# Last tile's stores of a fused attention and MLP kernel: two groups of 64 rows per transfer, the left columns of one half on their own

## The chip, the cores and the metric

The kernel runs on one core of a Trainium2 chip. The metric is device time: the microseconds that one execution takes on that core, as the median of three runs.

## The reference, cut to what matters

Efficient attention, then a two-layer MLP. `q`, `k` and `v` are float32 of shape (8, 8, 576, 64): batch, heads, sequence, head dimension. Per batch and head

- `q_s` is the softmax of `q` over the head dimension, `k_s` the softmax of `k` over the sequence;
- `kv = k_s^T v` (64 x 64), and the attention output is `q_s kv`.

The heads are laid side by side, which gives `x` of 4608 tokens by 512. Then `h = x w_in` (512 to 2048), `g = max(0.01 h, h)`, and the output is `g w_out` (2048 to 512): 4608 x 512 float32, 9.44 MB.

## The kernel before, in words

**Tiles.** The 4608 tokens are worked in nine tiles of 512 (`TT`). For each tile the attention output, transposed, is the right operand of layer 1; its result goes through the leaky ReLU and is the left operand of layer 2, whose result stands with tokens on the 128 partitions and 512 output columns. From tile 1 on layer 2 uses a scheme of seven products of half-size blocks in place of eight; tiles 7 and 8 use it for both layers. Each product is accumulated in PSUM by TensorE (`behind`, L922) and the quarters of the output are sums of products: some are kept in SBUF by ScalarE (`q...` words, L987 and L989), and the last addition of each quarter is one VectorE TENSOR_TENSOR that writes the output tile (`total`, L871).

**Order.** The order of the instructions is written out by hand: `SCORE` is a list of words for tiles 1 to 6, `WEAVE` (L816) one for tiles 7 and 8, and `of_tile` (L933) turns a word into instructions. Each engine runs its own instructions in that order; a semaphore holds one back until what it needs is done. The last words of `WEAVE` are

```
d21 P310 d22 d11 d120 P311 d121
```

`P310` and `P311` are the two halves of the last product for the second 128 rows. `d21`, `d22`, `d11`, `d120` and `d121` are the final sums on VectorE. The first digit behind the `d` names the half of the tile (2 is the second 256 rows, 1 the first), the second the columns (1 is the left 256, `low`; 2 the right 256, `high`). `d120` and `d121` are the right columns of the first half, split by 128 rows, because they wait for the last product.

**The output tile.** `rows_out(t, c)` is a float32 tile of 128 partitions x 2 x 512 for half `c` of tile `t`: the middle index (`sub`) is the group of 128 tokens, the partition is the token within it. Tokens are ordered by `(r, l)` within a batch, `r` one of 9 and `l` one of 64, and token `(r, l)` is row `9 l + r` of the batch in DRAM. So the 128 partitions of a `sub` hold two groups of 64 rows (`i` = 0 and 1: partitions 0 to 63, and 64 to 127), and a group's 64 rows lie 9 rows of 2,048 bytes apart in DRAM.

**Stores.** `put` (L724, its DMA at L728) stores a half of a tile: one DMA for each `sub` and each `i`, 64 rows of 2,048 bytes, 128 KB. In the last tile (`t == NT - 1`, tile 8) `issue` (L1007) gives the DMAs of `i` = 0 to SyncE (SP) and those of `i` = 1 to ScalarE (ACT); in the other tiles all go to SP. For the last tile the calls are

- at L1003, as soon as `d21` and `d22` are both issued: four stores for the second half (c = 1);
- at L992, after `d120` and again after `d121`: two stores each, for one `sub` of the first half (c = 0), whole rows. `d11` has already written the left columns of both.

That is eight stores, four on SP and four on ACT. Behind them in each queue stands only the end of the program (L1112 for the compiler's closing waits), where SP waits for every DMA to land before all engines sign off.

Of the kernel before, what the change touches and what calls it, by code (L numbers as in the profile page):

```python
# [19 lines left out]
L = 64  # L20
# [5 lines left out]
def kernel(  # L26
# [13 lines left out]
    B, H, S, D = q.shape  # L40
# [9 lines left out]
    TT = 512  # L50
# [673 lines left out]
    def put(t, osb, c, os, subs=both, issue=(nc.sync, nc.sync)):  # L724
        for sub in subs:
            for i in range(2):
# [2 lines left out]
                    out=out_r[b, r0 // L, :, os], in_=osb[c][i * L : (i + 1) * L, sub, os]  # L729
                )  # L730

    spare = {}

    def spare_tile(key, shape, dtype):
# [120 lines left out]
    def rows_out(t, c):  # L855
        if (t, c) not in ot:
            ot[t, c] = osb_pool.tile([P, 2, O], FP32, name="out_sb")
        return ot[t, c]
# [74 lines left out]
    def of_tile(t, word):  # L933
        kind, p = word.split("_")[0], int(word[-1])
        k0 = word[0]
        out_bank = lambda x, i=0: bank[x, t, "out", i][0]
        if k0 == "u":
            j = int(word[1]) * NK + p
            c0 = L if t == 1 else 0
            bank["U", t, j] = psB_pool.tile([P, TT - c0], FP32, name="ph", tag=BANK_TAG)  # L940
            layer1(j, bank["U", t, j], t * TT + c0, TT - c0)
        elif k0 == "l" and "_" not in word:
            h = int(word[1])
            leaky(g_of(t, p // 2)[:, h, p % 2, L if t == 1 else 0 : TT], bank["U", t, h * NK + p])
        elif k0 == "m":
            ahead(t, int(kind[1]), p)
        elif k0 == "P" and len(word) == 3:
            s, p = int(word[1]), int(word[2])
            if p == 0:
                bank["O", t, s] = psO_pool.tile([P, O], FP32, name="pout")  # L950
            for i in range(4 * p, 4 * p + 4):
                layer2(bank["O", t, s], [g_of(t, kk) for kk in range(p + 1)], s, ORDER[i], i == 0, i == NF - 1)
        elif k0 == "P":
            behind(t, *(int(c) for c in word[1:]))
        elif k0 == "s":
            nc.scalar.copy(out=fill(t, kind, p), in_=bank["Z" if kind == "s5" else "X", t, p])  # L956
        elif k0 == "c":
            x, held = {"c11": ("Y", "s1"), "c22": ("X", "s5"), "c12": ("Z", "s6")}[kind]
            held = empty(t, held, p)
            total(fill(t, kind, p), bank[x, t, p], held)  # L960
        elif k0 == "l":
            z = {"l11": "a1", "l12": "a2", "l21": "b1", "l22": "b2"}[kind]
            if kind == "l11" and t >= WOVEN:
                c = empty(t, "c11", p)
                nc.vector.scalar_tensor_tensor(
                    out=corner(t, p, z), in0=c, scalar=LEAKY_SLOPE, in1=c, op0=ALU.mult, op1=ALU.max
                )
            else:
                leaky(corner(t, p, z), bank["X", t, p] if kind == "l21" else empty(t, "c" + kind[1:], p))
        elif k0 == "n":  # L970
            i = int(kind[1])
            h = p if t in PAIRED else p // 2
            if (t, h, i) not in nt:
                nt[t, h, i] = sum_pool.tile([P, 2, 2, HT], BF16, name=f"gs{i + 1}{h}")
            if t in PAIRED:
                o, (x, y) = nt[t, h, i], (corners(t, h, z) for z in SUB[kind])
            else:
                o, (x, y) = nt[t, h, i][:, place(t, p)], (corner(t, p, z) for z in SUB[kind])
            nc.vector.tensor_tensor(out=o, in0=x, in1=y, op=ALU.subtract)  # L979
        elif word == "q21":  # L980
            nc.scalar.copy(out=rows_out(t, 1)[:, :, low], in_=out_bank("X"))
        elif k0 == "q":
            i = int(word[1])
            if (t, i) not in keep:
                keep[t, i] = fill(t, word, 0) if i == 4 else keep_tile(i)
            if len(word) == 3:
                nc.scalar.copy(out=keep[t, i][:, p : p + 1], in_=out_bank("Z", p))  # L987
            else:
                nc.scalar.copy(out=keep[t, i], in_=out_bank({1: "X", 4: "V", 5: "Z", 6: "X"}[i]))  # L989
        elif word in ("d120", "d121"):  # L990
            total(rows_out(t, 0)[:, p : p + 1, high], out_bank("Z", p), keep[t, 6][:, p : p + 1])
            put(t, {0: rows_out(t, 0)}, 0, whole, [p], issue(t))  # L992
        elif k0 == "d" and len(word) == 2:
            o = rows_out(t, p // 2)[:, p % 2]
            move(nc.scalar if p < 2 else nc.vector, o, bank["O", t, p])
        elif k0 == "d":
            c, os, x, i = {"11": (0, low, "Y", 1), "12": (0, high, "Z", 6), "22": (1, high, "X", 5), "21": (1, low, "X", 4)}[word[1:]]
            total(rows_out(t, c)[:, :, os], out_bank(x), keep[t, i])
            if i == 4:
                empty(t, "q4", 0)  # L1000
            made[t, word] = True
            if t >= WOVEN and c == 1 and (t, "d21") in made and (t, "d22") in made:
                put(t, {1: rows_out(t, 1)}, 1, whole, both, issue(t))  # L1003
        else:
            put(t, {p: rows_out(t, p)}, p, whole)

# [110 lines left out]
```

## Time and profile before

| | us |
|---|---|
| median of 3 runs | 268.75 (268.65 to 268.89) |
| the profiled execution | 268.51 |
| its span, first to last recorded instruction | 266.7 |
| TensorE busy in the span | 256.2 (96%) |
| VectorE, ScalarE busy | 223.1, 193.1 |

The granted TensorE clock was 0.995 over the span. The profiled execution is 0.24 us below the median of the three runs, and 1.8 us of it lies outside the span.

A row of the timeline or of a group gives start and duration in us, the engine, the line of the kernel, the operation, and the tiles (out<-in) with their shapes and count. "SPq" and "ACTq" rows are DMA issues on the queues of SyncE and ScalarE: their duration is that of the issuing instruction, not of the transfer. The DMA view of a stretch has two rows of 40 slices (busy share of the 16 DMA engines in tenths, and GB/s), then the packets of each queue: q1 is SP's, q10 is ACT's, q14 and q8 are fetches of instructions. The share behind a queue is the sum of its packets' durations over 16 engines times the stretch; packets that start in a stretch count in full, so a share can pass 100%. "Us to landing" is from the start of the issue until the last of the transfer's semaphore counts has come in.

### The profile page before, as it was taken

How to read it: one execution, taken by the hardware profiler on the slowest of the kernel's cores; microseconds unless marked ns; L12 is line 12 of the kernel's file. 1: busy time of each engine (PE TensorE's matmuls, PEld its weight loads, DVE VectorE, ACT ScalarE, POOL GpSimd, SP SyncE). 2: the span in 40 equal slices, each digit the busy share in tenths (PEclk: the TensorE clock that was granted, in tenths of full speed). 3: DMA queues.
4: the chain of work that ended last, by engine and by line, in shares of the span. 5: the costliest groups of instructions: out<-in, count | busy, mean ns of one | idle time of the engine just before them, and what ended most of it. 6: DMA issues, size and time to landing. Idle time of an engine off the chain costs nothing.

```text
span 266.7 us, 6315 instructions
## 1 busy us (share of the span) xinstructions
PE 256.2 (96%) x2559; PEld 188.4 (71%) x2570; DVE 223.1 (84%) x390; ACT 193.1 (72%) x367; POOL 64.2 (24%) x45
## 2 busy tenths in 40 slices
PE   7689999999999999999999999999999999999992
PEld 3167744457864686458888864588888788888882
DVE  2997899699999999989798969786999579779952
ACT  4977893689579769797469766878996589628920
POOL 2484442160038100000930191058000000000000
PEclk9999999999999999999999999999999999999998
DMA  7999999996895299299409766463028160042004
GB/s 242 343 210 360 314 209 268 316 327 244 187 396 218 48 240 339 78 179 332 172 4 243 279 187 247 95 81 75 2 51 179 41 140 0 2 96 64 1 2 159
DMA packets 37646, 46.49 MB, mean 174 GB/s; under 512 B 18160, under 2 KB 21232, under 8 KB 37616
## 3 DMA queue, kind: packets, MB, share of 16 engines
q1 hardware_dynamic: 32976, 36.64, 47.7%
q0 software_dynamic: 4320, 8.91, 13.4%
q10 hardware_dynamic: 320, 0.52, 0.6%
q8 instruction: 20, 0.33, 0.5%
q14 instruction: 10, 0.08, 0.1%
HBM read 36.70 MB, written 9.44 MB: 173 GB/s over the span
## 4 chain that ended last, share of the span: by engine, by line
PE 84%; DMA 6%; ACT 2%; DVE 1%; issue 1%; POOL 0%; ACTq 0%; POOLq 0%
PE acc L922 37%; PE ph L491 29%; PE ph L892 14%; DMA w_in_sb<-in_moe_w_in_dram 3%; DMA qX<-qe 3%; PE po L436 2%; PE pkv L294 2%; ACT ke L201 1%; DVE k_raw L378 1%; PE pout L516 1%; ACT vb L211 1%; ACT qe L264 0%; POOL w_in_sb L129 0%; DVE out_sb L871 0%; POOL gate L574 0%
## 5 line engine op out<-in xcount | busy, mean ns | idle before, releaser
L491 PE MATMUL ph<-xT,w_in_sb 128*128 128x256 bf16 (+3 forms) x505 | 85.8, 325 | 0.8 <-DMA w_in_sb<-in_moe_w_in_dram 0.2
L491 PEld LDWEIGHTS <-w_in_sb 128*128 128x128 bf16 x512 | 49.6, 98 | 32.9 <-issue 0.6
L500 ACT ACTIVATE gj<-ph 128x512 bf16<-128x512 f32 (+2 forms) x116 | 60.7, 573 | 15.5 <-PE ph L491 10.8
L922 PEld LDWEIGHTS <-gs 128*128 128x128 bf16 x512 | 49.5, 98 | 7.0 <-issue 1.0
L256 POOL TENSOR_TENSOR q_raw<-q_raw,qmax 128x2304 f32<-128x2304 f32 (+3 forms) x10 | 30.8, 3086 | 89.3 <-ACT xT L427 55.2
L922 PEld LDWEIGHTS <-gj 128*128 128x128 bf16 x384 | 37.3, 98 | 6.1 <-issue 0.4
L922 PE MATMUL acc<-w_out_sb,gj 128*128 128x256 bf16 x256 | 32.2, 273 | 0.0
L922 PE MATMUL acc<-wsum,gs 128*128 128x256 bf16 x256 | 30.6, 273 | 0.0
L922 PE MATMUL acc<-w_out_sb,gs 128*128 128x256 bf16 x256 | 30.4, 273 | 0.0
L979 DVE TENSOR_TENSOR gs<-gj 128x512 bf16<-128x512 bf16 (+1 forms) x56 | 24.6, 456 | 1.9 <-ACT gj L500 1.7
L871 DVE TENSOR_TENSOR part_spare<-ph,part_spare 128x512 f32<-128x512 f32 x36 | 23.5, 686 | 2.8 <-PE ph L892 2.5
L979 DVE TENSOR_TENSOR gs<-gj,gs 128x512 bf16<-128x512 bf16 (+1 forms) x56 | 24.7, 458 | 0.9
L956 ACT COPY part_spare<-ph 128x512 f32<-128x512 f32 x36 | 19.3, 592 | 8.1 <-PE ph L892 7.7
L427 ACT CAST xT<-po 128x320 bf16<-128x320 f32 (+2 forms) x47 | 19.0, 482 | 7.9 <-PE po L436 7.6
L871 DVE TENSOR_TENSOR out_sb<-acc,keep 128x512 f32<-128x512 f32 (+1 forms) x26 | 16.5, 645 | 9.3 <-ACT xT L427 6.1
L273 DVE TENSOR_REDUCE qsum<-qe 128x36 f32<-128x2304 bf16 (+4 forms) x11 | 19.7, 1793 | 3.2 <-ACT qe L264 3.1
L264 ACT ACTIVATE qe<-q_raw 128x2304 bf16<-128x2304 f32 (+4 forms) x11 | 16.8, 1526 | 6.8 <-POOL q_raw L256 6.8
L280 DVE TENSOR_TENSOR qe<-qe,qrec 128x2304 bf16<-128x2304 bf16 (+4 forms) x12 | 21.2, 1763 | 0.2
L225 DVE TENSOR_REDUCE qmax<-q_raw 128x36 f32<-128x2304 f32 (+4 forms) x11 | 19.6, 1791 | 1.4 <-DMA q_raw<-in_q_dram 1.4
L989 ACT COPY keep<-acc 128x512 f32<-128x512 f32 x22 | 12.8, 585 | 10.9 <-PE acc L922 9.9
L892 PEld LDWEIGHTS <-fs_spare 128*128 128x128 bf16 x192 | 18.8, 98 | 2.2
L892 PE MATMUL ph<-xs_spare,fs_spare 128*128 128x256 bf16 x144 | 19.2, 273 | 0.0
(86 smaller groups left out, 313.9 us busy)
## 6 DMA issues: line engine op xcount, KB each, us to landing
out_dram<-out_sb SPq DMA_DIRECT2D x68, 128.0 KB, 3.3
q_raw<-in_q_dram SPq DMA_DIRECT2D x6, 1152.0 KB, 8.2
v_raw<-in_v_dram SPq DMA_DIRECT2D x6, 1152.0 KB, 7.9
k_raw<-in_k_dram SPq DMA_DIRECT2D x5, 1152.0 KB, 7.2
w_in_sb<-in_moe_w_in_dram POOLq DMA_DIRECT2D x4, 512.0 KB, 7.9
w_out_sb<-in_moe_w_out_dram POOLq DMA_DIRECT2D x3, 512.0 KB, 16.0
k_raw<-in_k_dram SPq DMA_DIRECT2D x2, 576.0 KB, 5.4
v_raw<-in_v_dram SPq DMA_DIRECT2D x2, 576.0 KB, 7.4
```

Source lines behind the costliest of these rows:

```text
L225: nc.vector.tensor_reduce(out=m, in_=st[b]["q"][:, :, rs], axis=AX.X, op=ALU.max)
L256: eng.tensor_tensor(out=qs, in0=qs, in1=st[b]["qmax", rs.start].unsqueeze(3).to_broadcast([P, HL, n, D]), op=ALU.subtract,)
L273: nc.vector.reduce_sum(out=qsum, in_=st[b]["qe"][:, rs], axis=AX.X)
L280: eng.tensor_tensor(out=qes, in0=qes, in1=st[b]["qrec", rs.start].unsqueeze(3).to_broadcast([P, n, HL, D]), op=ALU.mult,)
L427: eng.copy(out=o, in_=i)
L491: nc.tensor.matmul(ph[:, n0:n1], lhsT=w_in_sb[:, i, j * P : (j + 1) * P], rhs=xT[:, i, (c0 + n0) % NX : (c0 + n0) % NX + n1 - n0], start=( ...
L500: nc.scalar.activation(out=o, in_=ph, func=AF.Prelu, alpha=LEAKY_SLOPE)
L871: nc.vector.tensor_tensor(out=o, in0=x, in1=y, op=ALU.add)
L892: nc.tensor.matmul(bank[x, t, p][:, jj], lhsT=lhs(k, 2 * p + jj), rhs=rhs[:, k], start=(first and k == 0 and jj == 0), stop=(k == 1), skip ...
L922: nc.tensor.matmul(b[:, at_], lhsT=lhs(k)[:, sub * P : (sub + 1) * P], rhs=rhs[:, k], start=(first and k == 0 and at_ == 0), stop=(k % (NK ...
L956: nc.scalar.copy(out=fill(t, kind, p), in_=bank["Z" if kind == "s5" else "X", t, p])
L979: nc.vector.tensor_tensor(out=o, in0=x, in1=y, op=ALU.subtract)
```

## The change

Only tile 8 changes, and only its stores; no sum and no product is touched.

- A new helper `put_both` stores the two subs of a half in one DMA for each `i`: 64 partitions x 2 subs, so both groups of 64 rows that lie on these partitions.
- The second half (c = 1) is stored by two such DMAs of 256 KB, whole rows, in place of four of 128 KB.
- Behind `d11` two DMAs store the left 256 columns of the first half: 64 partitions x 2 subs x 1,024 bytes, 128 KB each.
- The stores behind `d120` and behind `d121` take the right 256 columns alone: 64 rows x 1,024 bytes, 64 KB each, two DMAs each.

There are eight stores before and after, four on each queue.

```diff
+    def put_both(t, osb, c, os, issue):
+        b, r0 = divmod(t * TT + c * HT, S)
+        for i in both:
+            issue[i].dma_start(
+                out=out_r[b, r0 // L + i : r0 // L + i + 3 : 2, :, os].rearrange("r l o -> l r o"),
+                in_=osb[c][i * L : (i + 1) * L, :, os],
+            )
...
         elif word in ("d120", "d121"):
             total(rows_out(t, 0)[:, p : p + 1, high], out_bank("Z", p), keep[t, 6][:, p : p + 1])
-            put(t, {0: rows_out(t, 0)}, 0, whole, [p], issue(t))
+            put(t, {0: rows_out(t, 0)}, 0, high if t == NT - 1 else whole, [p], issue(t))
...
             if t >= WOVEN and c == 1 and (t, "d21") in made and (t, "d22") in made:
-                put(t, {1: rows_out(t, 1)}, 1, whole, both, issue(t))
+                if t == NT - 1:
+                    put_both(t, {1: rows_out(t, 1)}, 1, whole, issue(t))
+                else:
+                    put(t, {1: rows_out(t, 1)}, 1, whole, both, issue(t))
+            if t == NT - 1 and word == "d11":
+                put_both(t, {0: rows_out(t, 0)}, 0, low, issue(t))
```

## The prediction

> **What bounds the kernel now.** All that the change can move lies behind the last sums, so I read the end of the trace. First the span of the page, then the chain of work that ended last from 255 us on, and VectorE's rows in the timeline, the final sums.
>
> ```profile
> span 266.7 us, 6315 instructions
> ```
> ```profile
> 254.97 7.00 PE acc L922 x64
> ...
> 261.99 0.42 DVE out_sb L871
> ```
> ```profile
> 259.60 1.34 DVE L871 TENSOR_TENSOR out_sb<-acc,keep 128x512 f32<-128x512 f32 x2
> ...
> 261.12 0.42 DVE L871 TENSOR_TENSOR out_sb<-acc,keep 128x256 f32<-128x256 f32 x1 [0.18 <-PE acc L922]
> ```
>
> TensorE runs without a gap into the last sum, d121, which ends at 261.99 + 0.42 = 262.41. d22 and d11 are the pair that ends at 259.60 + 1.34 = 260.94; d120 ends at 261.54. The span goes on to 266.7: 4.3 us in which only stores run. No earlier instruction changes, so this tail is all there is to win, and only part of it: next the issues, each from the timeline, with the landings of the first and the last pair from the DMA view.
>
> ```profile
> 260.31 0.47 SPq L728 DMA_DIRECT2D out_dram<-out_sb  x1
> 260.31 0.55 ACTq L728 DMA_DIRECT2D out_dram<-out_sb  x1
> 260.82 0.60 SPq L728 DMA_DIRECT2D out_dram<-out_sb  x1
> 260.91 0.80 ACTq L728 DMA_DIRECT2D out_dram<-out_sb  x1
> 261.57 0.50 SPq L728 DMA_DIRECT2D out_dram<-out_sb  x1
> 262.10 0.47 ACTq L728 DMA_DIRECT2D out_dram<-out_sb  x1
> 262.44 0.47 SPq L728 DMA_DIRECT2D out_dram<-out_sb  x1
> 262.67 0.55 ACTq L728 DMA_DIRECT2D out_dram<-out_sb  x1
> ```
> ```profile
> out_dram<-out_sb SPq DMA_DIRECT2D x1, 128.0 KB, 2.3
> out_dram<-out_sb ACTq DMA_DIRECT2D x1, 128.0 KB, 2.6
> ```
> ```profile
> out_dram<-out_sb SPq DMA_DIRECT2D x1, 128.0 KB, 3.0
> out_dram<-out_sb ACTq DMA_DIRECT2D x1, 128.0 KB, 3.1
> ```
>
> The first pair, on idle DMA engines, lands 2.3 and 2.6 us after its issue. The last pair needs 3.0 and 3.1, so ACT's last store lands at 262.67 + 3.1 = 265.77 and is the end; 0.97 us of closing work follows up to 266.7, and 1.8 us lie outside the span (268.51 - 266.7). Against the first pair the last is late by 0.5 to 0.7 us: it stands in a queue. The DMA view from 261.4 to 265.5 shows the queue.
>
> ```profile
> DMA  6699499899999459988977798979999998831000
> GB/s 160 180 260 260 100 220 320 320 380 400 420 400 380 160 200 280 240 260 320 300 280 260 200 280 240 300 200 300 320 340 380 380 400 300 340 140 60 20 20 0
> DMA packets 641, 1.06 MB, mean 258 GB/s; under 512 B 128, under 2 KB 128, under 8 KB 640
> ...
> q1 hardware_dynamic: 320, 0.52, 40.6%
> q10 hardware_dynamic: 320, 0.52, 38.9%
> q14 instruction: 1, 0.01, 1.2%
> ```
>
> The engines move data from the first slice (1.1 us after the first issue) to about 265.4. One engine-stretch is 16 x 4.1 = 65.6 us, so the stores took 0.795 x 65.6 = 52.2 us of engine time, 3.26 us for each of 16 engines, out of some 4.0 us in which they moved anything. **The tail is bound by the DMA engines, at four fifths full, and not by the issue of the last store.** The 512 data packets (641 less 128 small ones and the fetch) cost 102 ns each with their share of the small ones. One engine also carries the q14 packet: 0.012 x 65.6 = 0.79 us more.
>
> **The change part by part.**
>
> *Second half in two transfers.* The issues at 260.82 and 260.91 vanish, and their 256 KB come with those at 260.31, so the engines have them 0.5 to 0.6 us sooner. The bytes and the 256 packets stay. The issue itself could take longer for a pattern of two dimensions; the nearest row is the load below (L99), which has 128 partitions x 4 heads and was issued in 0.47 us, as the stores are. I take no extra cost; the upper end is the 0.80 us of ACT's second issue, which would push ACT's next one by 0.3 us, into time where it already waits for d11.
>
> *Left columns behind d11.* d11 ends at 260.94, so this pair takes the slots of the vanished one: SP, free from 260.78, now waits 0.17 us for d11, and ACT, free from 260.86, some 0.1 us. Behind the wait stand only the two right-column pairs, whose data come at 261.54 and 262.41. With issues of 0.50 to 0.80 us the queues are free again at 261.5 to 261.8, against 261.42 and 261.71 now: the third pair can go by about 261.6 and the last at 262.44. VectorE, TensorE and GpSimd issue nothing here.
>
> *Right columns alone.* 64 KB in place of 128 KB behind each sum. The other halves, 256 KB in all, leave 0.6 to 1.7 us sooner than they did (260.95 against 261.57 to 262.67).
>
> *Smaller packets.* This is what the change pays: 256 packets of 2 KB become 512 of 1 KB. The trace shows no 1 KB store. Three rows bound it: a stretch of 1 KB loads (3.0 to 3.6 us), 2 KB stores with a full queue (54.6 to 56.2 us), and 2 KB stores issued by SP alone, one after another (237 to 242 us).
>
> ```profile
> q1 hardware_dynamic: 218, 0.22, 105.8%
> ```
> ```profile
> DMA packets 376, 0.62 MB, mean 390 GB/s; under 512 B 72, under 2 KB 72, under 8 KB 376
> ...
> q1 hardware_dynamic: 376, 0.62, 105.3%
> ```
> ```profile
> DMA packets 614, 1.03 MB, mean 206 GB/s; under 512 B 112, under 2 KB 112, under 8 KB 614
> ...
> q1 hardware_dynamic: 614, 1.03, 88.7%
> ```
>
> A 1 KB load packet takes 1.058 x 16 x 0.6 / 218 = 46.6 ns. A 2 KB store packet takes 1.053 x 16 x 1.6 / 304 = 89 ns in the full queue and 0.887 x 16 x 5.0 / 502 = 141 ns in the lone stream. So 1 KB costs about 0.525 of 2 KB at its best (46.6 / 89), and I take that share of the tail's 102 ns: 54 ns. The ends are 46.6 ns, and 75 ns: half of the 141 and a little for the pieces.
>
> The work after is (256 x 102 + 512 x 54) / 16 = 1.63 + 1.73 = 3.36 us per engine, **+0.10 us**. Against that stand the idle engine time and what the earlier issues fill of it: the stretch from 262.8 to 264.2, where the GB/s row sags to 160 to 320.
>
> ```profile
> q10 hardware_dynamic: 120, 0.21, 51.3%
> q1 hardware_dynamic: 85, 0.14, 27.7%
> q14 instruction: 1, 0.01, 3.5%
> ```
>
> The engines are 82.5% busy there, so 0.175 x 1.4 = **0.25 us** is lost; I count all of it as won, since half a megabyte is then queued before 262.8. The sum is +0.10 - 0.25 = **-0.15 us**. It can't be much more while the engine with the q14 packet keeps it: that engine's work is 3.36 + 0.79 = 4.15 us from 261.4, which ends near 265.5 as now. So the last landing goes from 265.77 to about 265.6, the profiled execution from 268.51 to 268.36, and the median, 0.24 us above it, from 268.75 to **268.6**.
>
> [...]
>
> **The rivals.**
>
> *Faster: the tail is latency after all.* If packets run at the full-queue prices (89 and 46.6 ns), the work is (256 x 89 + 512 x 46.6) / 16 = 2.91 us and done by 264.4, and the last pair is bound by its own latency: 262.44 to 262.67 plus 2.6 us, less about 0.1 for half the bytes, is 264.95 to 265.2 in place of 265.77. That is 0.6 to 0.8 us won: about 268.1. For it speaks that 262.0 to 262.7 runs at 320 to 420 GB/s; against it the 17.5% of idle engine time from 262.8 on, when both queues hold work, and the q14 packet. I give it 0.23.
>
> *Slower: small packets with the halves in lock-step.* Each transfer still reads 64 partitions; a stream of such transfers ran at 141 ns a packet (206 GB/s), not 89. A transfer twice as long leaves the two halves alternating less often, and the 1 KB pieces pay that pace: at 75 ns, (256 x 102 + 512 x 75) / 16 = 4.03 us of work, +0.77 us if no idle time is won: 269.5. It decides (beyond 0.54 us) from 68 ns a piece if nothing is won, from 75 if the 0.25 are. The first slices of the tail (100 to 260 GB/s with SP's transfer alone) are for it; the full-queue row at 390 GB/s against. 0.18.
>
> *Not what it says: an added wait.* Left and right columns interleave in the same tile and rows. If d120 or its store had to wait for the left columns' landing (260.95 + 2.6 = 263.55, against 261.54), two more issues and a landing follow: 264.1 + 2.3 = 266.4 for a waiting store, +0.65 us, and up to +1.3 if VectorE waits: 269.4 to 270.05. Against it: two loads fill interleaved parts of `q_raw`, and the reduction of the first started at 4.67, before the second, issued at 3.51, landed 8.9 us later. 0.05.
>
> ```profile
> 4.67 1.28 DVE L233 TENSOR_REDUCE nmax<-q_raw 128x8 f32<-128x512 f32 x2 [4.67 <-DMA q_raw<-in_q_dram]
> ```
> ```profile
> 3.51 0.47 SPq L99 DMA_DIRECT2D q_raw<-in_q_dram  x1
> ```
> ```profile
> q_raw<-in_q_dram SPq DMA_DIRECT2D x1, 640.0 KB, 8.9
> ```
>
> *A transfer on few engines.* If the two groups rather than the 64 rows were what is spread, 2 of 16 engines would carry 128 packets: 64 x 89 ns = 5.7 us for the first transfer alone, 1.1 us after its issue, and 64 x 46.6 = 3.0 us more for the next, and the last packets end near 270.1 in place of 265.4: about 273. The 1 KB loads above have an inner dimension of 4 and kept all 16 engines busy (105.8%), and the helper puts the 64 rows outermost. 0.02. [...]
>
> **How the numbers follow.** Forecast 0.52, faster rival 0.23, slower 0.18, added wait 0.05, few engines 0.02. 0.2% of 268.75 is 0.54 us, about what a measurement of this kernel can tell from no change. The forecast's own range, from all idle time won at 46.6 ns a piece to none won at 65, is 268.35 to 269.2, all within it. So faster is 0.23, same 0.52, slower 0.25. The range takes in the faster rival down to 268.0 and the slower one up to 269.5, and leaves out the last two, 0.07.
>
> **What would show it.** Right: two issues at 260.31 on SP and ACT, two at about 260.95; d120 and d121 still end near 261.54 and 262.41; the stores' engine time 52 to 55 us; 1 KB packets at 50 to 58 ns; a last landing near 265.6 on the engine that had the fetch. The sum is wrong if engine time falls below 48 us (faster rival) or passes 60 us (slower), if a row of waits shows SP, ACT or VectorE held by a DMA of `out_sb`, or if the first transfers take over 4 us to land. If q14's packet falls before 261 or behind the last store, up to 0.4 us more can be won than I count.

## The result, and the profile after

The changed kernel takes **269.78 us** (median of 8 runs, 269.43 to 269.94) where the kernel before took 268.86 (8 runs, 268.65 to 269.16) on the same chip. The ratio is 1.0032, with a 95% interval from 1.0022 to 1.0041: slower, by about 0.9 us. The profiled execution took 269.46 us.

The page's span first, then VectorE's last two sums in the timeline.

```profile
span 267.7 us, 6328 instructions
```
```profile
261.08 0.42 DVE L879 TENSOR_TENSOR out_sb<-acc,keep 128x256 f32<-128x256 f32 x1 [0.18 <-PE acc L930]
261.95 0.42 DVE L879 TENSOR_TENSOR out_sb<-acc,keep 128x256 f32<-128x256 f32 x1 [0.45 <-PE acc L930]
```

The span is 1.0 us longer. The last sum ends at 261.95 + 0.42 = 262.37, no later than before. So all of the loss stands behind it, in the stores. The issues in the timeline (start, duration of the issuing instruction), and from the DMA view the landings of ACT's first and last transfer:

```profile
260.27 0.65 SPq L735 DMA_DIRECT2D out_dram<-out_sb  x1
260.27 0.74 ACTq L735 DMA_DIRECT2D out_dram<-out_sb  x1
261.02 0.60 SPq L735 DMA_DIRECT2D out_dram<-out_sb  x1
...
262.53 1.25 SPq L728 DMA_DIRECT2D out_dram<-out_sb  x1
262.56 1.18 ACTq L728 DMA_DIRECT2D out_dram<-out_sb  x1
263.84 0.56 ACTq L728 DMA_DIRECT2D out_dram<-out_sb  x1
```
```profile
out_dram<-out_sb ACTq DMA_DIRECT2D x1, 256.0 KB, 4.5
...
out_dram<-out_sb ACTq DMA_DIRECT2D x1, 64.0 KB, 2.8
```

Line 735 is the new helper. A merged store takes 0.65 and 0.74 us to issue, not 0.47 and 0.55, and ACT's first lands 4.5 us behind its issue. The last lands at 263.84 + 2.8 = 266.6, where before it was 265.8. The DMA view from 261.4 to 266.2:

```profile
DMA  0498997899899799999998979999977996221000
GB/s 0 119 239 188 222 256 171 171 222 171 137 171 222 188 324 290 375 282 273 273 299 273 333 265 350 350 359 307 376 256 265 333 290 214 86 94 34 17 17 0
DMA packets 897, 1.06 MB, mean 220 GB/s; under 512 B 128, under 2 KB 640, under 8 KB 896
...
q1 hardware_dynamic: 448, 0.52, 43.1%
q10 hardware_dynamic: 448, 0.52, 36.3%
```

For a third of the stretch the engines are busy (7 to 9 tenths) and move only 120 to 260 GB/s. The stores' engine time is (0.431 + 0.363) x 16 x 4.8 = 61.0 us, where before it was 52.2. The next fences show where: the stretch in which SP's transfer ran alone, in the kernel before (261.4 to 262.0), and in the changed one (261.5 to 262.9, then 262.9 to 263.5).

```profile
DMA packets 59, 0.12 MB, mean 201 GB/s; under 512 B 0, under 2 KB 0, under 8 KB 59
...
q1 hardware_dynamic: 59, 0.12, 90.9%
```
```profile
DMA packets 124, 0.25 MB, mean 181 GB/s; under 512 B 0, under 2 KB 0, under 8 KB 124
...
q1 hardware_dynamic: 124, 0.25, 89.3%
```
```profile
DMA packets 100, 0.17 MB, mean 287 GB/s; under 512 B 16, under 2 KB 16, under 8 KB 100
...
q10 hardware_dynamic: 80, 0.16, 87.8%
q1 hardware_dynamic: 20, 0.01, 7.7%
```

In the first two there is no q10 row at all: **ACT's data move only when SP's first transfer is through**, though both were issued together. ACT's first piece starts at 262.02 us before and 262.92 after, the last piece of SP's first transfer at 262.11 and 262.93. That transfer runs at 201 and 181 GB/s with engines that look 90% busy (0.909 x 16 x 0.6 us / 59 = 148 ns a piece before, 0.893 x 16 x 1.4 / 124 = 161 after), and the change made it twice as long. The 1 KB pieces, in contrast, are cheap; 264.0 to 265.4 holds little else:

```profile
DMA packets 495, 0.44 MB, mean 313 GB/s; under 512 B 82, under 2 KB 487, under 8 KB 494
...
q10 hardware_dynamic: 270, 0.24, 54.1%
q1 hardware_dynamic: 224, 0.19, 40.1%
```

That is 0.942 x 16 x 1.4 / 412 = 51 ns with their share of the small packets.

**Where the time went.** From the first issue to the last landing, the tail, was 5.45 us and is 6.42: +0.97. From all packets of the two traces: the first data come 1.32 us behind the first issue and not 1.12 (+0.20); the data packets alone take 59.8 us of engine time and not 51.0 (+8.8 / 16 = +0.55 for each engine); what is left over, the engines' idle time and the way from the last data to the landing, is 0.89 and not 0.96 us (-0.07); and the last engine ends 0.47 us behind the fifteen others and not 0.18 (+0.29). By size: 256 pieces of 2 KB at 139 ns (99.6 before, the mean of all 512) add 10.2 us, and 512 pieces of 1 KB at 47.2 ns cost 1.3 us less than the 256 of 2 KB in their place.

### The profile page after: what moved, and what is told of

Same layout as the page of the kernel before. It is cut to its first block, busy times and chain, and to the rows that moved or that the text cites. A ratio compares the mean times of both kernels' runs of the same rounds, so it can differ in the third digit from the quotient of the medians.

```text
span 267.7 us, 6328 instructions
## 1 busy us (share of the span) xinstructions
PE 257.5 (96%) x2570; PEld 188.7 (70%) x2570; DVE 223.3 (83%) x390; ACT 193.0 (72%) x367; POOL 64.2 (24%) x45
## 4 chain that ended last, share of the span: by engine, by line
PE 84%; DMA 6%; ACT 2%; DVE 1%; issue 0%; POOL 0%; ACTq 0%; POOLq 0%
PE acc L930 37%; PE ph L491 29%; PE ph L900 14%; DMA w_in_sb<-in_moe_w_in_dram 3%; DMA qX<-qe 3%; PE po L436 2%; PE pkv L294 2%; ACT ke L201 1%; DVE k_raw L378 1%; PE pout L516 1%; ACT vb L211 1%; ACT qe L264 0%; POOL w_in_sb L129 0%; DVE out_sb L879 0%; POOL gate L574 0%
## 5 line engine op out<-in xcount | busy, mean ns | idle before, releaser
L256 POOL TENSOR_TENSOR q_raw<-q_raw,qmax 128x2304 f32<-128x2304 f32 (+3 forms) x10 | 30.8, 3086 | 89.3 <-DMA out_dram<-out_sb 38.9
L997 ACT COPY keep<-acc 128x512 f32<-128x512 f32 x22 | 12.8, 585 | 11.2 <-PE acc L930 10.2
```

Source lines behind the costliest of these rows:

```text
L256: eng.tensor_tensor(out=qs, in0=qs, in1=st[b]["qmax", rs.start].unsqueeze(3).to_broadcast([P, HL, n, D]), op=ALU.subtract,)
```

## The experiments

**Theory 1**: a transfer that reads 64 of the 128 partitions moves at half the rate while it is alone, and the merge lengthens the stretch in which it is alone. **Theory 2**: the many 1 KB pieces, or the issues that they hold up (1.18 and 1.25 us above), cost the time. A third suspect is the fetch of instructions (q14), one packet of 8 KB late in the tail: at 263.06 us for 0.79 us before, at 264.82 for 0.31 after.

All experiments in one table. Tail, ACT's first data behind SP's, engine time of data packets and the lag of the last engine are from each kernel's one trace. The lag is how far the last transfer's last semaphore count comes behind the one before it, which is read as the last engine behind the others: each store of the tail has 16 counts, the 16th comes 0.02 to 0.05 us behind the 15th in the stores that land ahead of the fetch (and within 0.25 us of its start), and 0.18 to 0.55 us (before) or 0.30 to 0.66 us (after) in every one that lands later. The medians stand beside the kernel before on the same chip; "-" marks a kernel that was timed once.

| kernel | tail, us | ACT behind SP, us | engine us | lag, us | median (before) | ratio, 95% |
|---|---|---|---|---|---|---|
| before | 5.45 | 0.59 | 51.0 | 0.18 | 268.75 | |
| after | 6.42 | 1.34 | 59.8 | 0.47 | 269.78 (268.86) | 1.0032, 1.0022 to 1.0041 |
| e1 merge only | 6.42 | 1.33 | 57.8 | 0.51 | 269.80 (268.77) | 1.0043, 1.0029 to 1.0056 |
| e2 split only | 5.66 | 0.58 | 52.8 | 0.19 | 269.36 (268.77) | 1.0022, 1.0012 to 1.0032 |
| e3 right columns once | 6.30 | 1.34 | 60.4 | 0.50 | 269.71 (268.77) | 1.0037, 1.0025 to 1.0050 |
| e4 lone stores | 5.32 | 0.58 | 50.7 | 0.05 | 268.71 (268.77) | - |
| e5 merge on SP | 5.77 | ACT first, by 0.59 | 52.5 | 0.52 | 268.85 (268.43) | 1.0018, 1.0009 to 1.0026 |
| e6 merge on ACT | 5.64 | 0.58 | 53.2 | 0.11 | 268.62 (268.43) | 1.0011, 1.0002 to 1.0019 |
| e7 before, 16 SP stores more | 5.17 | 0.58 | 50.8 | 0.04 | 268.87 (268.43) | 1.0015, 1.0006 to 1.0024 |
| e9 after, 16 SP stores more | 5.94 | 1.34 | 59.6 | 0.02 | 269.74 (268.43) | 1.0045, 1.0032 to 1.0058 |
| e8 second half in four, early | 6.10 | 0.28 | 57.6 | 0.02 | 268.89 (268.47) | 1.0023, 1.0013 to 1.0033 |
| e10 SP stores more, late | 5.46 | 0.58 | 50.9 | 0.30 | 268.46 (268.47) | 1.0001, 0.9992 to 1.0010 |
| e11 full-width probe | 5.50 | 0.58 | 50.8 | 0.09 | 268.79 (268.47) | - |
| e12 before, ScalarE copies | 5.27 | 0.63 | 52.1 | 0.08 | 268.30 (268.47) | 0.9993, 0.9985 to 1.0002 |
| e13 before, VectorE copies | 5.55 | 0.65 | 50.9 | 0.34 | 268.45 (268.47) | 0.9998, 0.9990 to 1.0007 |
| e14 after, ScalarE copies | 6.12 | 1.38 | 60.8 | 0.03 | 269.09 (268.47) | 1.0021, 1.0012 to 1.0031 |
| e15 after, VectorE copies | 6.82 | 1.38 | 61.5 | 0.61 | 269.81 (268.47) | 1.0051, 1.0039 to 1.0063 |
| e16 merge over 128 partitions | 15.09 | 3.21 | 58.5 | 0.85 | 278.24 (268.57) | 1.0359, 1.0345 to 1.0373 |
| e17 the same, spread | 5.16 | 0.65 | 47.4 | 0.02 | 268.26 (268.46) | 0.9992, 0.9983 to 1.0001 |

### The parts one by one: e1, e2, e3

e1 has only the merged second half; first the edit of the changed kernel:

```diff
-            put(t, {0: rows_out(t, 0)}, 0, high if t == NT - 1 else whole, [p], issue(t))
+            put(t, {0: rows_out(t, 0)}, 0, whole, [p], issue(t))
...
-            if t == NT - 1 and word == "d11":
-                put_both(t, {0: rows_out(t, 0)}, 0, low, issue(t))
```

> Only the first part of the change: the second half in two transfers of 256 KB; the first half's stores as before (six transfers, 512 pieces of 2 KB). Theory 1 (lone halves: a transfer that reads 64 partitions moves about 200 GB/s while it is alone, and ACT's first waits behind SP's, now 1.4 us in place of 0.6): most of the loss is here, slower than before by 0.5 us or more (ratio 1.002 or above). Theory 2 (pieces: 768 in place of 512 pieces stand in the queues and the issues are held until those ahead have gone): no issue longer than 0.8 us, the last pair issued by 262.7, the time within 0.3 us of before or faster.

e2 has only the split into left and right columns:

```diff
-                if t == NT - 1:
-                    put_both(t, {1: rows_out(t, 1)}, 1, whole, issue(t))
-                else:
-                    put(t, {1: rows_out(t, 1)}, 1, whole, both, issue(t))
+                put(t, {1: rows_out(t, 1)}, 1, whole, both, issue(t))
```

> Only the second part: the second half in four transfers of 128 KB as before, the left columns of the first half behind d11, the right columns on their own (ten transfers, 768 pieces). Theory 1: ACT's first data 0.6 us behind SP's as before and no loss from it, the time within 0.3 us of before. Theory 2: issues of 1 us and more on both queues, the last issue at 263.5 or later, slower than before by 0.6 us or more.

e3 is the changed kernel with the right columns stored once, behind the last sum:

```diff
-            put(t, {0: rows_out(t, 0)}, 0, high if t == NT - 1 else whole, [p], issue(t))
+            if t < NT - 1:
+                put(t, {0: rows_out(t, 0)}, 0, whole, [p], issue(t))
+            elif p == 1:
+                put_both(t, {0: rows_out(t, 0)}, 0, high, issue(t))
```

> The changed kernel, but the right columns of both groups go in one transfer for each queue behind the last sum (six transfers, 768 pieces). Theory 1: nothing at the front changes, so slower than before by about 0.9 us as the change is. Theory 2, if it is the number of pieces: the third issue on each queue comes at 262.4 and is held until about 263.7 as in the change, and the time stays within 0.3 us of it; if it is the number of transfers waiting, the third issue isn't held (under 0.8 us) and 0.5 us or more come back.

The DMA view of e1, for its tail (261.6 to 266.4), then for its first stretch (261.7 to 263.0):

```profile
DMA packets 609, 1.06 MB, mean 220 GB/s; under 512 B 96, under 2 KB 96, under 8 KB 608
...
q1 hardware_dynamic: 304, 0.52, 41.9%
q10 hardware_dynamic: 304, 0.52, 34.5%
```
```profile
DMA packets 121, 0.25 MB, mean 191 GB/s; under 512 B 0, under 2 KB 0, under 8 KB 121
...
q1 hardware_dynamic: 121, 0.25, 92.4%
```

The merge alone, without a single 1 KB piece, has the whole loss: the same tail of 6.42 us, the same stretch of SP alone at 191 GB/s. Its last issue starts 2.30 us behind its first, as in the kernel before (2.36), where the changed kernel's starts 3.57 behind, and it ends no sooner for that. So theory 2 falls as the cause of the loss: neither the pieces nor the held-up issues are needed for it. e3 says the same with a third layout. e2's tail is 0.21 us longer than before; its median, though, is 0.59 us up. The rest, some 0.4 us, stands ahead of the tail in its one profile (first issue at 260.65, where the traces of before, after, e1 and e3 have 260.27 to 260.46). The same TensorE instruction at 8 us, in the kernel before and in e2, shows it already, 0.38 us apart and some 250 us ahead of the split's stores:

```profile
8.04 0.33 PE L352 MATMUL kT<-identf,kmax 128*128 128x128 f32 x1 [0.93 <-DVE kmax L160]
```
```profile
8.42 0.33 PE L352 MATMUL kT<-identf,kmax 128*128 128x128 f32 x1 [0.46 <-DVE kmax L160]
```

So it isn't a cost of the stores in that trace; what it is stays open, and so does why eight of e2's nine runs are above 269.1 us. The two parts don't add up to the whole either (1.0043 and 1.0022 against 1.0032), so the split's own effect on the median stays open.

### The rate of a lone transfer: e4, e11

e4 leaves tile 8 as before and puts the new forms in tile 6, where SP stores with no other traffic (and tile 7's first half as the change has it in tile 8):

```diff
...
-            put(t, {p: rows_out(t, p)}, p, whole)
+            if t == 6 and p == 0:
+                put_both(t, {0: rows_out(t, 0)}, 0, whole, issue(t))
+            elif t == 6:
+                for os in (low, high):
+                    put(t, {1: rows_out(t, 1)}, 1, os)
+            else:
+                put(t, {p: rows_out(t, p)}, p, whole)
```

> Tile 8 as before; tiles 6 and 7, where SP alone stores and the DMA engines are otherwise nearly idle, are used as a probe: the first half of tile 6 in two transfers of 256 KB (2 KB pieces, two groups of rows), its second half in eight of 64 KB (1 KB pieces), tile 7's first half in left columns merged and right columns apart. If a lone transfer is bound by the bytes that 64 partitions can give (Theory 1), 256 KB takes 1.2 us and 1 KB pieces take about 70 ns, 64 KB some 0.3 us. If it is bound by the number of pieces (about 10 ns each, Theory 2), 256 KB takes 1.3 us too, but 64 KB of 1 KB pieces takes 0.6 us, and its pieces are drawn out to 130 ns or stand apart.

The DMA view of e4 at 213.0 to 214.2 (a 256 KB store of 64 partitions, alone) and at 218.4 to 220.3 (64 KB stores of 1 KB pieces, one after another):

```profile
DMA packets 117, 0.24 MB, mean 200 GB/s; under 512 B 0, under 2 KB 0, under 8 KB 117
...
q1 hardware_dynamic: 117, 0.24, 97.3%
```
```profile
DMA packets 240, 0.20 MB, mean 104 GB/s; under 512 B 48, under 2 KB 240, under 8 KB 240
...
q1 hardware_dynamic: 240, 0.20, 40.5%
```

Alone, a merged store runs at 200 GB/s, 0.973 x 16 x 1.2 / 117 = 160 ns a piece. The 1 KB pieces cost 0.405 x 16 x 1.9 / 192 = 64 ns with their small packets; at 104 GB/s the engines are idle 60% of the time.

e11 adds two probe stores that read all 128 partitions:

```diff
+            if t == 6 and p == 0:
+                nc.sync.dma_start(out=out[T - 2 * P : T - P], in_=rows_out(6, 0)[:, 0])
+            if t == 6 and p == 1:
+                nc.sync.dma_start(
+                    out=out[T - 4 * P : T - 2 * P].rearrange("(s p) o -> p s o", s=2), in_=rows_out(6, 1)
+                )
```

> A probe: SP stores tile 6's first half once more behind its four stores, one group of 128 rows from all 128 partitions (256 KB) and later both groups of the second half (512 KB), into rows of the output that tile 8 writes over. If a lone transfer is slow because it reads 64 partitions (Theory 1), the 256 KB go in 0.7 to 0.8 us at 84 to 100 ns a piece, the 512 KB in 1.4 to 1.6. If every lone transfer is slow, whatever it reads, 150 ns a piece and 1.3 and 2.6 us.

The DMA view of e11 at 213.0 to 215.0 (the kernel's own stores of 64 partitions) and at 218.5 to 219.6 (the 512 KB probe):

```profile
DMA packets 247, 0.42 MB, mean 211 GB/s; under 512 B 48, under 2 KB 48, under 8 KB 246
...
q1 hardware_dynamic: 246, 0.41, 88.4%
```
```profile
DMA packets 229, 0.45 MB, mean 408 GB/s; under 512 B 10, under 2 KB 10, under 8 KB 229
...
q1 hardware_dynamic: 229, 0.45, 105.0%
```

The same queue moves 408 GB/s from 128 partitions and 211 from 64, with engines that look about as busy (105.0% and 88.4%): 1.05 x 16 x 1.1 / 219 = 84 ns a piece against 0.884 x 16 x 2.0 / 198 = 143. In the half-width stores each piece was slower; engines were not left unused.

### How long SP keeps ACT out: e5, e6, e8

e5 merges only SP's two stores of the second half, e6 only ACT's, by a helper that takes the queue to merge:

```diff
+    def put_some(t, osb, c, os, issue, merged):
+        b, r0 = divmod(t * TT + c * HT, S)
+        for sub in both:
+            for i in both:
+                if i != merged:
+                    put_one = out_r[b, r0 // L + i + 2 * sub, :, os]
+                    issue[i].dma_start(out=put_one, in_=osb[c][i * L : (i + 1) * L, sub, os])
+                elif sub == 0:
+                    issue[i].dma_start(
+                        out=out_r[b, r0 // L + i : r0 // L + i + 3 : 2, :, os].rearrange("r l o -> l r o"),
+                        in_=osb[c][i * L : (i + 1) * L, :, os],
+                    )
...
+                    put_some(t, {1: rows_out(t, 1)}, 1, whole, issue(t), 0)
```

(e6 has 1 as the last argument.)

> The kernel before, with SP's two stores of the second half merged into one of 256 KB; ACT's two stay at 128 KB. Theory 1 (lone halves: on every engine SP's first transfer is worked off before ACT's first, at 150 ns a piece of 2 KB): ACT's first data come 1.3 to 1.4 us behind SP's as in the change, and most of the loss stays, +0.6 us or more. Theory 3 (the two-dimensional pattern or the merging itself costs, on whichever queue): half of the loss, about +0.5 us, here and the same with ACT's merged.

> The mirror: ACT's two stores of the second half merged, SP's two at 128 KB as before. Theory 1: ACT's first data come 0.6 us behind SP's as before, SP's second transfer waits behind ACT's 256 KB, which go at 85 to 100 ns a piece (read ahead while SP's went out); loss within 0.3 us of before. Theory 3: about +0.5 us, the same as with SP's merged.

e5 missed its aim: ACT's transfer went first (issued in 0.57 us, SP's in 0.65), and its 128 KB are what then ran alone, at 201 GB/s from 261.6 to 262.2 us. In both kernels the first transfer is 128 KB, the other queue comes 0.58 to 0.59 us behind it, and more than half of the loss is gone: 1.0018 and 1.0011 against 1.0043 with both merged. These two medians don't exclude theory 3 of the expectations by themselves (half of the loss for either merge would be about 1.0021, and e5's interval holds that); e17 below does. That ACT's pieces are read ahead while SP's go out, as e6's expectation has it, no run shows.

e8 makes the first transfers smaller and earlier: left columns of the second half behind `d21`, right columns behind `d22`, twelve stores in all.

```diff
-            if t >= WOVEN and c == 1 and (t, "d21") in made and (t, "d22") in made:
+            if t == NT - 1 and word in ("d21", "d22"):
+                put(t, {1: rows_out(t, 1)}, 1, os, both, issue(t))
+            if WOVEN <= t < NT - 1 and c == 1 and (t, "d21") in made and (t, "d22") in made:
                 put(t, {1: rows_out(t, 1)}, 1, whole, both, issue(t))
```

> The kernel before, with the second half's left columns stored behind d21 and its right columns behind d22 (eight stores of 64 KB in place of four of 128 KB, twelve in all). If the tail is bound by the bytes that the DMA engines move from the first store on, data start 0.6 us sooner and up to 0.6 us are won, at least 0.2; if small transfers hold the queues up (issues of 0.6 us, six on each queue from 259.7 on, the last pair issued at 263 or later), nothing is won or 0.3 us lost.

ACT now comes 0.28 us behind SP. So the second queue's wait was 0.28, 0.59 and 1.34 us for first transfers of 64, 128 and 256 KB: in step with their size. What makes it wait for all of the first transfer, no run shows. The kernel is slower all the same (1.0023). It starts sooner, but its data take 57.6 us of engine time and its last store leaves 3.66 us behind the first; which of the two costs it wasn't tried apart.

### The fetch at the end: e7, e9, e10, e12 to e15

Where the fetch of 8 KB of instructions falls into the tail, one engine often ends late (a lag of up to 0.61 us, e16 with its few engines apart), but not always: e8 and e17 have a fetch there and a lag of 0.02 us. e7 and e9 are the kernels before and after with the stores of tiles 4 and 5 in two pieces, so that SP has 16 more instructions:

```diff
-            put(t, {p: rows_out(t, p)}, p, whole)
+            for os in (low, high) if t in (4, 5) else (whole,):
+                put(t, {p: rows_out(t, p)}, p, os)
```

> The kernel before, with 16 more store instructions on SP long before the tail (tiles 4 and 5 stored in left and right columns), so that SP's fetch of 8 KB of instructions should fall before the tail. If the fetch is SP's and holds one DMA engine back, no q14 packet lies behind 257 us, the last counts of each transfer come in together (within 0.1 us, not 0.2 to 0.5), and 0.2 to 0.4 us are won. If the fetch is another engine's, it stays at 263 and nothing is won. If the stores of tiles 4 and 5 matter themselves, the loss shows ahead of 240 us.

> The changed kernel with the same 16 more store instructions. If the fetch adds to the change's loss (one engine's counts came 0.5 us behind the others there, 0.2 in the kernel before), 0.3 to 0.5 us come back and the loss against before is 0.4 to 0.7 us; Theory 1 alone (the fetch is no part of it): the loss stays at 0.9 us.

The fetch left the tail in both, and the last engine's lag with it (0.04 and 0.02 us). The medians didn't fall: the pieces themselves cost time ahead of the tail, as the first issues at 260.93 and 261.09 show against 260.31 and 260.27. e10 has them later, in tiles 6 and 7:

```diff
+            put(t, {0: rows_out(t, 0)}, 0, high if t == NT - 2 else whole, [p], issue(t))
...
+                for os in (low, high) if t < NT - 1 else (whole,):
+                    put(t, {1: rows_out(t, 1)}, 1, os, both, issue(t))
+            if t == NT - 2 and word == "d11":
+                put(t, {0: rows_out(t, 0)}, 0, low, both, issue(t))
...
+            for os in (low, high) if t == 6 else (whole,):
+                put(t, {p: rows_out(t, p)}, p, os)
```

> The kernel before, with 16 more store instructions on SP in tiles 6 and 7 (left and right columns apart), where SP has no loads left to issue; tile 8 as before. If the 0.6 us that the same number of stores cost in tiles 4 and 5 came from SP being late with loads and transposes there, the first issue of the tail comes at 260.3 to 260.4 as before; the fetch then lies ahead of the tail, the tail from first issue to last landing is 5.2 us in place of 5.3 to 5.45, and 0.1 to 0.3 us are won. If any 16 stores cost it, the first issue comes 0.5 us later and the time is 0.3 us over before.

The fetch stayed, as the row of e10's DMA view shows (261.2 to 265.6), so it doesn't go by SP's instructions:

```profile
q14 instruction: 1, 0.01, 1.1%
```

e12 and e14 are the kernels before and after with eight tiny copies on ScalarE late in tile 8; e13 and e15 have eight on VectorE ahead of `d21`:

```diff
+    idle = const_pool.tile([P, 1], BF16)
...
                 nc.scalar.copy(out=keep[t, i][:, p : p + 1], in_=out_bank("Z", p))
+                if t == NT - 1 and p == 1:
+                    for _ in range(8):
+                        nc.scalar.copy(out=idle, in_=ident[:, 0:1])
```
```diff
...
+            if t == NT - 1 and word == "d21":
+                for _ in range(8):
+                    nc.vector.tensor_copy(out=idle, in_=ident[:, 0:1])
             total(rows_out(t, c)[:, :, os], out_bank(x), keep[t, i])
```

> The kernel before, with eight copies of one element per partition on ScalarE behind its last keep copy, in the 2.8 us in which it has nothing to do before the stores. If the fetch that holds one DMA engine back in the tail is ScalarE's, it comes ahead of 261, the tail from first issue to last landing is 5.2 us in place of 5.3 to 5.5, and 0.1 to 0.3 us are won against before. If it is another engine's, it stays at about 263 and the time is within 0.1 us of before.

> The kernel before, with eight copies of one element per partition on VectorE ahead of d21, in the 3 us in which it has nothing to do. If the fetch is VectorE's, it comes ahead of 261, the tail is 5.2 us and 0.1 to 0.3 us are won; if not, the fetch stays at 263 and the time within 0.1 us of before (or d21 comes up to 0.3 us later if the copies don't fit).

> The changed kernel with the same eight copies on ScalarE. If the fetch is ScalarE's: tail 5.9 us in place of 6.4, 0.4 to 0.5 us come back, the rest of the loss (0.2 us of later first data and 0.4 of the first transfers' lone stretch, some 0.5 us together) stays. If not: as the change, 0.9 us over before.

> The changed kernel with the same eight copies on VectorE. If the fetch is VectorE's: tail 5.9 us in place of 6.4, 0.4 to 0.5 us come back and some 0.5 us of loss stay. If not: as the change, 0.9 us over before.

e12's copies in its timeline, then the data queues of e12 (261.2 to 265.4) and e14 (261.4 to 266.3), which have no row of q14:

```profile
257.29 1.77 ACT L991 COPY idle<-ident 128x1 bf16<-128x1 bf16 x8
```
```profile
DMA packets 640, 1.05 MB, mean 250 GB/s; under 512 B 128, under 2 KB 128, under 8 KB 640
```
```profile
DMA packets 896, 1.05 MB, mean 214 GB/s; under 512 B 128, under 2 KB 640, under 8 KB 896
```

With ScalarE's copies the tail has no fetch (the last is at 248.8 and 248.9 us, where the kernels before and after have one too, at 248.67 and 248.34), and with VectorE's it has one (263.4 and 265.3 us), so I take it for ScalarE's. e7 and e9 fit: in their traces ScalarE has three instructions more as well (457 against 454, 458 against 455, the added ones waits on semaphores), and in e10, where the fetch stayed, it has none more.

With the fetch out of the tail, the changed kernel is 0.79 us above its partner (269.09 and 268.30, e14 and e12) and 0.87 us (e9 and e7). With it there, they are 0.92 us apart, and 1.36 us in e15 and e13. So most of the loss is there without the fetch, which can add to it. e15 missed its expectation: its loss is 1.34 us and not 0.9, and its tail is 0.40 us longer than the change's. Why isn't known.

### The same merge at full width: e16, e17

e16 merges the second half the other way: SP and ACT have one transfer of 256 KB each, as with the change, but each reads all 128 partitions.

```diff
+    def put_full(t, osb, c, os, subs, issue):
+        for sub in subs:
+            b, r0 = divmod(t * TT + c * HT + sub * P, S)
+            issue[sub].dma_start(
+                out=out_r[b, r0 // L : r0 // L + 2, :, os],
+                in_=osb[c][:, sub, os],
+            )
...
-                put(t, {1: rows_out(t, 1)}, 1, whole, both, issue(t))
+                (put_full if t == NT - 1 else put)(t, {1: rows_out(t, 1)}, 1, whole, both, issue(t))
```

> The kernel before, with the second half of tile 8 stored in two transfers as the change does, 256 KB each, one on SP and one on ACT, but cut the other way: each covers one group of 128 tokens from all 128 partitions (128 rows of 2,048 bytes), not 64 partitions with two groups. Same bytes, same count of transfers, same pieces; only the partitions that one transfer reads differ. Theory 1 (half the partitions: a transfer that reads 64 of them moves about 200 GB/s alone, and merging lengthens that stretch): SP's first transfer runs at 390 to 410 GB/s and is done in about 0.65 us, so ACT's first data come 0.5 to 0.7 us behind SP's and not 1.34; 2 KB pieces cost 85 to 105 ns; the stores' engine time falls to 45 to 50 us; the tail from first issue to last landing is 5.0 to 5.4 us against 6.42 with the change's merge; median 267.9 to 268.6 against about 268.5 before. Rival (long transfers as such, or one queue's turn at the engines): ACT's first data again 1.2 us or more behind, tail 6.0 us or more, median 269.2 or above. Third outcome: if the 128 rows are spread over only 2 of the 16 engines because the DRAM side has a group dimension of 2 outermost, 64 pieces of about 85 ns run on each, 5.4 us for a transfer, the share in the first microseconds stays near 2 of 16 engines and the end moves several us out, to 270 or more.

It came out at 278.24 us. The DMA view of e16 from 268 to 274 shows why:

```profile
DMA  1111110111111101111111111111111111111111
...
q10 hardware_dynamic: 100, 0.20, 8.6%
q1 hardware_dynamic: 58, 0.11, 4.6%
```

(0.086 + 0.046) x 16 = 2.1 engines work. The DRAM side's outermost dimension is the 2 groups of rows, and about that many engines worked here; with the 64 rows outermost, in the changed kernel, SP's first transfer kept 16 engines 89.3% busy. e17 puts the 64 rows outermost on the DRAM side. It is a probe of time alone: it leaves out the order of the rows, so that within each of the two transfers nearly all of the 128 rows land in another's place.

```diff
-                out=out_r[b, r0 // L : r0 // L + 2, :, os],
+                out=out_r[b, r0 // L : r0 // L + 2, :, os].rearrange("r l o -> l r o"),
```

> As e16 (second half of tile 8 in two transfers of 256 KB from all 128 partitions each), but with the 64 rows outermost on the DRAM side, so that 64 and not 2 is the slowest dimension there and all 16 engines should share it. The price is that the 256 rows of the last half land in another order among themselves: every piece is still a row of 2,048 bytes from one partition to one row of the output, and count, size and place of the transfers are those of the change's merge. Theory 1 (half the partitions): ACT's first data 0.5 to 0.7 us behind SP's, SP's first transfer alone at 390 to 410 GB/s, engine time 45 to 51 us, tail 4.9 to 5.4 us, median 267.9 to 268.7 against 268.5 before. Rival (the merge itself, at any width): ACT's first data 1.2 us or more behind, tail 6 us or more, median 269.2 or above.

The DMA view of e17 for the tail (261 to 266), at 261.3 to 261.9, where SP's first transfer is alone, and at 261.8 to 262.4, where ACT's data have joined:

```profile
DMA packets 609, 1.06 MB, mean 211 GB/s; under 512 B 96, under 2 KB 96, under 8 KB 608
...
q1 hardware_dynamic: 304, 0.52, 32.4%
q10 hardware_dynamic: 304, 0.52, 27.9%
q14 instruction: 1, 0.01, 0.4%
```
```profile
DMA packets 108, 0.22 MB, mean 369 GB/s; under 512 B 0, under 2 KB 0, under 8 KB 108
...
q1 hardware_dynamic: 108, 0.22, 94.8%
```
```profile
DMA packets 139, 0.25 MB, mean 420 GB/s; under 512 B 16, under 2 KB 16, under 8 KB 139
...
q10 hardware_dynamic: 82, 0.17, 71.8%
q1 hardware_dynamic: 57, 0.08, 37.4%
```

Alone, SP's first transfer has pieces of 0.948 x 16 x 0.6 / 108 = 84 ns. Against e1, with the same count and size of transfers and the same 256 rows of DRAM, the width differs, and the loss is gone: 268.26 us against 269.80, 0.9992 of the kernel before (0.9983 to 1.0001) against 1.0043. ACT comes 0.65 us behind SP and not 1.33, the data cost 47.4 us of engine time and not 57.8, and the tail is 5.16 us and not 6.42 (0.49 us of the difference is the lag, 0.51 against 0.02). The first data are still 1.27 us behind the issue, so that 0.15 to 0.20 us belongs to the longer transfer and not to its width. **Theory 1 holds: the merge loses by the 64 partitions.**

One difference more goes with the width. Both full-width stores write rows that lie together in DRAM (e11 one run of rows, e17 neighbours in pairs), the half-width ones rows that lie apart. The distance alone isn't the cause: the prediction's row at 54.6 to 56.2 has stores of 64 rows that lie 9 apart, from both halves of the partitions in turn, and runs at 390 GB/s. A lone full-width store of rows that lie apart, on all 16 engines, wasn't run.

Merging two stores of 128 KB into one of 256 KB did not pay on 64 partitions (e1, 1.0043 of the kernel before) and cost nothing that was measured on 128 (e17, 0.9992).

No kernel here is shown to beat the one before: e12 at 0.9993 and e17 at 0.9992 are lowest, both intervals include no change, and e17 isn't a kernel to use.

## Why the prediction was wrong

The forecast was 268.6 us, 0.15 less than before. Measured were 269.78, 0.92 more than before on the same chip and above the range, which ended at 269.5.

- **Second half in two transfers**: the step that failed. I took no extra cost, "the bytes and the 256 packets stay", and the data 0.5 to 0.6 us sooner. The bytes did stay, but the pieces went from 99.6 to 139 ns (+10.2 us of engine time, 0.64 for each engine), mostly because the stretch of one half-width transfer alone, at 148 to 161 ns a piece, went from 0.59 to 1.34 us. ACT's first data came 0.95 us later (2.66 us behind their issue, 1.71 before), not sooner. The issue I priced at 0.47 us, by a load that reads DRAM; it took 0.65 and 0.74, and the first data 0.20 us with it.
- **Idle won, -0.25 us**: nothing was won. From the first data to the end of the last, 3.96 us before and 4.48 after, the engines work 3.31 and 3.83 us on average, so they idle 0.65 us in both. More queued bytes didn't fill the gaps.
- **Smaller packets**: 54 ns (+0.10 us) was too much. The 1 KB pieces took 47.2 ns, 51 with small packets: next to the lower bound, and a saving of 1.3 / 16 = 0.08 us.
- **The engine with the fetch**: I expected it to set the end near 265.5. The fetch moved: from 263.06 to 264.82, and the last engine was 0.47 us late and not 0.18. In e14, with no fetch in the tail, it is 0.03 us late.
- **The left columns behind `d11`** were issued at 261.02 on SP (260.95 foreseen), but the last pair left at 262.53 to 263.84, not at 262.44. e1, without this, has the same tail.
- **The slower rival** came nearest: 269.5 us against 269.78, by over 60 us of engine time, as its sign named (61.0). It named the 141 ns of the half-width stream and the longer turns of the two halves; it put the price on the 1 KB pieces, though, and those were cheap. The price belonged to the 2 KB pieces of the merged transfers, so that its nearness is partly luck. With 256 pieces at 139 ns in place of 102 in the sum, 0.59 us more for each engine, the forecast would have been 269.2 before the later first data, and 269.4 with them.
- **The faster rival** fell with the engine time. **The added wait** did not occur, as d120 and d121 kept their times and no sum and no store waited for a DMA of `out_sb`; only the closing wait does. **Few engines** did not occur in the change (90% of 16 engines busy from the start), but e16 has just that, at 278.24 us.
- **That the tail is bound by the DMA engines and not by the last issue** was right, and e1 confirms it.

What stays open: some 0.4 us of e2's loss, which lie ahead of its tail; the longer tail of e15; whether a lone full-width store of rows that lie apart is as fast as those of e11 and e17; why the pieces of a lone half-width transfer are slow, since only the rate was measured, not what limits it; and what holds the second queue back until the first transfer is through.

## What to carry to other kernels

Before you merge stores, ask which partitions one transfer reads and what moves while it has the engines: from 64 partitions, alone, it held the rate at 181 to 211 GB/s with engines that looked 88 to 97% busy, and the other queue's data came 0.28 to 1.34 us later. A merge across all 128 partitions, with 64 rows outermost on the DRAM side, lost nothing (e17), but there the rows landed out of order; with the rows in order and the 2 groups outermost it had 2.1 engines at work (e16, 268 to 274 us). So the order of the rows on the partitions would have to be planned for it, which wasn't tried; without that, leave the transfers apart. A packet price from a mixed stretch (102 ns here) is no price for a stretch in which one transfer is alone (148 to 161 ns): price each stretch by its own row.

## What the runs showed of the hardware that was not expected

- Two transfers issued together on SP and ACT did not start together: the second queue's data waited 0.28, 0.59 and 1.34 us for first transfers of 64, 128 and 256 KB from 64 partitions (e8, before, after), and 0.65 us for one of 256 KB from 128 (e17).
- Which queue goes first isn't fixed: in e5, where SP's issue took 0.65 us and ACT's 0.57, ACT's data came first by 0.59 us; before and after, SP's took 0.47 and 0.65, ACT's 0.55 and 0.74, and SP's came first.
- From 64 partitions a piece of 1 KB cost half of one of 2 KB or less: 47.2 against 99.6 ns in the tails of after and before, 64 against 160 ns alone (e4). So the bytes were paid here, not the pieces.
- A fetch of 8 KB of instructions (q14) in the tail went with a late 16th count of the stores that landed behind it (0.18 to 0.55 us before, 0.30 to 0.66 after), which I read as one DMA engine held up. Where it fell into the tail the last engine ended 0.02 to 0.61 us behind the others (e16 apart); without it the lag was 0.02 to 0.08 us (e7, e9, e12, e14). With eight tiny instructions more on ScalarE the tail had none (e12, e14).
